# Another order of ScalarE's tasks around the block products of a mixture-of-experts layer

## Chip, cores and metric

The kernel runs on one core of one Trainium2 chip. The metric is the device time of one execution in microseconds (us), and the time before is the median of three runs.

## What is computed

Eight heads of retention (attention without softmax, with a decay matrix) over a batch of 8 sequences of 576 tokens make 4608 rows of 512 numbers. A router then sends each row to one of 8 experts, and each expert is a two-layer network. The second part fills the half of the program that this case is about.

```python
def _moe_ref(x, expert_emb, tau, w1, w2):        # x 4608x512, w1 8x512x1024, w2 8x1024x512
    ...
    expert_idx = np.argmax(logits, axis=1)
    ...
    for e in range(E):
        mask = expert_idx == e
        h = np.maximum(x[mask] @ w1[e], 0.0)
        out[mask] = gate_w[mask, None] * (h @ w2[e])
```

## The kernel before

**Stages.** The first 187 us compute retention, routing and the first layer of expert 0. From there the program alternates, expert by expert, between two stages that TensorE does back to back. The second layer of an expert (`mm2`, line 1150) goes over five tiles of 128 tokens, 24 matmuls each. The first layer of the next expert (`product`, line 1099) is a **block** of 28 block products of six matmuls each: 1 to 7 by block scheme, for each of four weight chunks, seven products in place of eight, in the hand-written sequence `ORDER`. Blocks 1 to 7 belong to experts 1 to 7. Every number is held as a high and a low part, so each operand is split before use: ScalarE casts the high part (line 999 for weights, 399 for tokens) and VectorE subtracts it for the low part (lines 1002 and 403).

**Accumulators.** Products 1, 6, 7 and 4 of one chunk add into the same PSUM tile `Y`. After products 1, 6 and 7 ScalarE copies the sum so far out of `Y` (`follow`, line 1115), and the next product of that chunk must not start before this copy is done. In `ORDER`, product 1 of chunk 0 stands at place 1 and product 6 of chunk 0 at place 5; product 7 of chunk 3 stands at place 25 and product 4 of chunk 3 at place 27. What is copied gets VectorE's additions (line 1111) and goes through the ReLU into `hs`, again as high (line 1070, ScalarE) and low (line 1065, VectorE).

**Weights.** The first layer's weights come in four chunks per expert. Three quarters of a chunk are used as they are (its **own** part, 768 columns). GpSimd makes four **sums** of its blocks (`w1sum`, line 1024, 1024 columns) into the one buffer `wsum`. Both parts are split, `w1hi`/`w1lo` with True for the own part and False for the sums. A chunk's sums may overwrite `wsum` only when the split of the chunk before has read it. The second layer's four chunks are split by `w2hi`/`w2lo`. All these chunks pass through two buffers (raw_72 and raw_78), and `wload` starts the next load in a buffer, on SP's queue, once VectorE has done `w2lo` or the own `w1lo` there.

**Tokens.** GpSimd gathers the five token tiles of the expert after next. For each one ScalarE makes a 16-bit copy (`xturn`, line 357, 128x1024), after which SP issues a DMA that transposes it (line 358). In the next second-layer stage ScalarE joins the halves (`xjoin`, line 364), VectorE forms sums (lines 375 to 382), and both split.

**What sets the order.** All engines run a hand-written order. `mm2_plan` lists what is done in the second-layer stage at its 15 steps (three per tile: after matmul 8, after matmul 16, and after the tile's eviction, line 1159, and its scatter to `out`, line 1160). `mm1_plan` lists what is done after the 1st to 28th product. Each engine works off its queue in this order, and the instruction at the head of a queue holds back all behind it.

Of the kernel before, what the change touches and what calls it, by code (L numbers as in the profile page):

```python
# [84 lines left out]
def retention_moe(ctx: ExitStack, tc: tile.TileContext, qk, kv, w1, w2, head, cst, out):  # L85
# [872 lines left out]
    with ExitStack() as moe:  # L958
# [218 lines left out]
        def mm2_plan(e):  # L1177
            n = e + 1
            if n == NE:
                return {0: [(count_beyond,)]}  # L1180
            plan = {
                0: [(xjoin, n, 0)],
                1: [(xsums, n, 0), (xhigh, n, 0), (w1sum, n, 0)],
                2: [(xlow, n, 0), (w1hi, n, 0, True), (xjoin, n, 1)],
                3: [(xsums, n, 1), (w1lo, n, 0, True), (xhigh, n, 1)],
                4: [(xlow, n, 1), (w1hi, n, 0, False), (xjoin, n, 2)],
                5: [(xsums, n, 2), (w1lo, n, 0, False), (xhigh, n, 2), (w1sum, n, 1)],
                6: [(xlow, n, 2), (w1hi, n, 1, True), (xjoin, n, 3)],
                7: [(xsums, n, 3), (w1lo, n, 1, True), (xhigh, n, 3)],
                8: [(xlow, n, 3), (w1hi, n, 1, False), (xjoin, n, 4)],  # L1190
                9: [(xsums, n, 4), (w1lo, n, 1, False), (xhigh, n, 4), (w1sum, n, 2)],
                10: [(xlow, n, 4), (w1hi, n, 2, True)],
                11: [(w1lo, n, 2, True), (w1hi, n, 2, False)],
                12: [(w1lo, n, 2, False)],
            }
            if n + 1 < NE:
                for i in range(CT):
                    plan[2 + 2 * i].append((gather, n + 1, i))
                plan[12].append((xturn, n + 1, 0))
                plan[14] = [(xturn, n + 1, 1)]  # L1200
            if e == 0:
                plan[0] = [(xturn, 1, 4)] + plan[0]
                plan[12] += [(gather_gates, 1)]
            return plan

        def mm1_plan(e):
            n = e + 1
            plan = {
                2: [(w2hi, e, 0)],
                3: [(w2lo, e, 0), (w1sum, e, 3)],  # L1210
                10: [(w2hi, e, 1)],
                11: [(w2lo, e, 1)],
                12: [(w1hi, e, 3, True)],
                13: [(w1lo, e, 3, True), (w1hi, e, 3, False)],
                15: [(w1lo, e, 3, False)],
                17: [(w2hi, e, 2)],
                18: [(w2lo, e, 2)],
                22: [(w2hi, e, 3)],
                23: [(w2lo, e, 3)],
            }  # L1220
            if n < NE:
                for i, k in ((2, 6), (3, 19), (4, 24)):
                    plan[k] = [(xturn, n, i)]
                plan[9] = [(gather_gates, n)]
            return plan

        b = B - 1
# [13 lines left out]
        for i in range(3):  # L1241
# [4 lines left out]
        plan = {  # L1246
            4: [(w2hi, 0, 0), (gates_exp,)],
            5: [(w2lo, 0, 0), (w2hi, 0, 1)],
            6: [(gates_sum,), (xprep, 0, 3), (xprep, 0, 4)],
            7: [(w2lo, 0, 1)],  # L1250
            8: [(gates_out,)],
            9: [(w2hi, 0, 2), (gather, 1, 3), (gather, 1, 4)],
            10: [(w2lo, 0, 2), (xturn, 1, 0)],
            11: [(w2hi, 0, 3)],
# [9 lines left out]
        for e in range(NE):  # L1264
            if e:
                plan = mm1_plan(e)
                for k, (n, i) in enumerate(ORDER, 1):
                    product(e, n, i)
                    follow(n, i)
                    run_tasks(plan, k)  # L1270
                settle_last()
                settle_last()
            plan = mm2_plan(e)
            for i in range(CT):
                if e * CT + i == NA - 1:
                    ntile = nc.values_load(ovt[0:1, 0:1], min_val=0, max_val=NO)
                mm2(e, i, lambda k: run_tasks(plan, 3 * i + k))
# [186 lines left out]
```

## Time and profile before

| | |
|---|---|
| median of three runs | 603.17 us (602.69 to 603.18) |
| profiled execution | 606.0 us, span 604.2 us |
| busy in the span: TensorE (PE) | 573.9 us, 95% |
| VectorE (DVE) | 407.6 us, 67% |
| ScalarE (ACT) | 384.7 us, 64% |
| GpSimd (POOL) | 309.3 us, 51% |
| granted TensorE clock | 0.995 |

One execution is profiled; it took 1.8 us more than its span, and 2.8 us more than the median. All times of rows are us from the start of the span. Matmuls are pipelined and their ends are modelled, so the time that a stall costs TensorE is read better from the length of a block than from the busy share.

### The profile page before, as it was taken

What the parts mean: (1) busy time and instruction counts of PE and PEld (TensorE: products, weight loads), DVE (VectorE), ACT (ScalarE), POOL (GpSimd) and SP (SyncE); (2) the same over time, 40 slices, a digit from 0 to 9 for tenths busy, and PEclk for the clock granted to TensorE, in tenths of its full rate; (3) what the DMA queues carried; (4) which work ended last, traced back from release to release, by engine and by line L of the source; (5) the groups of instructions that cost most, each with busy time, mean ns of one, the idle gap of its engine ahead of it and who ended that gap; (6) DMA issues with size and microseconds to landing.
All of it is one profiled execution on the core that took longest, in us unless ns stands there. A gap on an engine that the chain in (4) does not pass through costs nothing.

```text
span 604.2 us, 13056 instructions
## 1 busy us (share of the span) xinstructions
PE 573.9 (95%) x5096; PEld 510.5 (84%) x5096; DVE 407.6 (67%) x829; ACT 384.7 (64%) x718; POOL 309.3 (51%) x303
## 2 busy tenths in 40 slices
PE   8999999998999988998998999899989989999996
PEld 7788888887898878888887988888888879889985
DVE  3565777665775857685966868686868768687800
ACT  1344556554557868768877878687587778786511
POOL 4554544454346586378257635933782575245011
PEclk9999999998999999999999999999999999999999
DMA  9999999953467575437735655644376366533201
GB/s 327 395 333 345 382 369 353 395 186 94 152 189 178 168 166 132 119 126 173 172 104 156 168 122 170 160 132 126 116 172 160 104 181 156 117 105 99 69 36 46
DMA packets 72385, 109.58 MB, mean 181 GB/s; under 512 B 42330, under 2 KB 44030, under 8 KB 70528
## 3 DMA queue, kind: packets, MB, share of 16 engines
q1 hardware_dynamic: 62976, 86.53, 47.2%
q0 software_dynamic: 7680, 19.95, 10.3%
q10 hardware_dynamic: 1664, 2.23, 1.1%
q8 instruction: 41, 0.67, 0.4%
q14 instruction: 24, 0.20, 0.1%
HBM read 80.62 MB, written 19.94 MB: 166 GB/s over the span
## 4 chain that ended last, share of the span: by engine, by line
PE 41%; ACT 18%; DVE 18%; issue 13%; POOL 5%; DMA 4%; ACTq 0%; POOLq 0%; DVEq 0%
PE m L1150 9%; PE a L1099 5%; PE a L626 5%; PE m L709 4%; POOL wsum L1024 4%; ACT raw L364 4%; PE a L413 3%; PE m L790 3%; PE m L1099 3%; ACT raw L357 3%; DVE raw L375 2%; DVE hs L1065 2%; ACT hs L1070 2%; PE m L653 2%; DVE y L1111 2%
## 5 line engine op out<-in xcount | busy, mean ns | idle before, releaser
L1150 PE MATMUL m<-w2s,hs 128*128 128x512 f32 (+1 forms) x984 | 219.6, 384 | 0.0
L1150 PEld LDWEIGHTS m<-w2s,hs 128*128 128x128 f32 x984 | 181.2, 188 | 36.0
L1160 POOL DMA_INDIRECT out<-y,sid x40 | 48.0, 1200 | 97.8 <-ACT y L1159 85.2
L1024 POOL TENSOR_TENSOR wsum<-raw 128x256 f32<-128x256 f32 x56 | 47.4, 870 | 62.5 <-DMA raw<-w 25.8
L615 POOL TENSOR_TENSOR qkt<-qkt,gsb 128x448 f32<-128x448 f32 x32 | 37.0, 1174 | 58.5 <-PE a L626 47.7
L1099 PE MATMUL a<-xsb,w0s 128*128 128x320 f32 x324 | 56.7, 314 | 10.0 <-ACT y L1115 9.8
L1099 PEld LDWEIGHTS a<-xsb,w0s 128*128 128x128 f32 x324 | 49.0, 188 | 13.4 <-ACT y L1115 12.7
L1002 DVE TENSOR_TENSOR w2s<-raw,w2s 128x1024 fp32r<-128x1024 f32 x32 | 41.0, 1280 | 19.9 <-issue 10.9
L319 POOL DMA_INDIRECT raw<-xd,gid x40 | 39.4, 985 | 27.3 <-DVE xsb L403 16.8
L330 POOL DMA_INDIRECT gt<-gd,gid x40 | 43.7, 1092 | 18.3 <-issue 10.2
L1070 ACT ACTIVATE hs<-y 128x320 fp32r<-128x320 f32 x84 | 38.7, 472 | 22.4 <-DVE y L1111 20.8
L1111 DVE TENSOR_TENSOR y<-m,y 128x320 f32<-128x320 f32 x84 | 39.1, 484 | 18.1 <-ACT y L1115 15.0
L399 ACT CAST xsb<-raw 128x128 fp32r<-128x128 f32 x70 | 32.1, 459 | 27.5 <-DVE raw L382 26.5
L635 DVE TENSOR_TENSOR raw<-a,cd 128x512 f32<-128x512 f32 x64 | 39.9, 683 | 13.6 <-PE a L626 12.6
L375 DVE TENSOR_TENSOR raw<-raw 128x256 f32<-128x256 f32 x35 | 19.7, 562 | 43.1 <-ACT raw L364 41.3
L1065 DVE SCALAR_TENSOR_TENSOR hs<-y,hs 128x320 fp32r<-128x320 f32 x84 | 46.1, 563 | 3.3 <-ACT hs L1070 1.4
L1159 ACT ACTIVATE y<-m,gt 128x512 f32<-128x512 f32 (+1 forms) x41 | 27.5, 671 | 32.1 <-PE m L1150 32.1
L403 DVE TENSOR_TENSOR xsb<-raw,xsb 128x128 fp32r<-128x128 f32 x70 | 46.9, 702 | 1.1 <-ACT xsb L399 0.6
L364 ACT COPY raw<-raw 128x1024 uint16<-128x1024 uint16 x35 | 47.4, 1353 | 0.0
L1115 ACT COPY y<-a 128x320 f32<-128x320 f32 x84 | 34.9, 425 | 7.7 <-PE a L1099 3.8
L999 ACT CAST w2s<-raw 128x1024 fp32r<-128x1024 f32 x32 | 33.6, 1049 | 6.8 <-DMA raw<-w 6.6
L1099 PE MATMUL m<-xsb,w0s 128*128 128x320 f32 x216 | 37.6, 309 | 0.0
(176 smaller groups left out, 1117.6 us busy)
## 6 DMA issues: line engine op xcount, KB each, us to landing
raw<-w SPq DMA_DIRECT2D x64, 512.0 KB
qkt<-qk SPq DMA_DIRECT2D x28, 576.0 KB
xd<-y SPq DMA_DIRECT2D x36, 256.0 KB
vt<-kv SPq DMA_DIRECT2D x7, 1152.0 KB
kt<-kv SPq DMA_DIRECT2D x7, 1024.0 KB
qkt<-qk ACTq DMA_DIRECT2D x4, 288.0 KB
qkt<-qk SPq DMA_DIRECT2D x4, 288.0 KB
raw<-xd,gid POOLq DMA_INDIRECT x40
```

The lines of the kernel that those rows point to most:

```text
L330: nc.gpsimd.indirect_dma_start(out=g[:, i : i + 1], out_offset=None, in_=gd[:, :], in_offset=bass.IndirectOffsetOnAxis(ap=gid[:, a : a + 1 ...
L364: nc.scalar.copy(far.bitcast(U16).rearrange("p (n h) -> p h n", h=2), near.rearrange("p (h n) -> p h n", h=2))
L403: nc.vector.tensor_tensor(out=lo, in0=u, in1=hi.bitcast(F32), op=ALU.subtract)
L635: nc.vector.tensor_tensor(out=pm[:, h], in0=ps[h].rearrange("p (c n) -> p c n", c=NCH), in1=decay[:, 2 * p + h].unsqueeze(1).broadcast_to( ...
L1002: nc.vector.tensor_tensor(out=lo, in0=u, in1=hi.bitcast(F32), op=ALU.subtract)
L1024: nc.gpsimd.tensor_tensor(out=o, in0=x, in1=y, op=op)
L1065: nc.vector.scalar_tensor_tensor(out=lo, in0=part(src), scalar=0.0, in1=hi.bitcast(F32), op0=ALU.max, op1=ALU.subtract)
L1070: nc.scalar.activation(hi, part(src), AF.Relu)
L1099: nc.tensor.matmul(ps[:, :HC], w[:, ws, ka, d * P : (d + 1) * P], xop(kx, xsp)[:, d, :], start=(n in (1, 2, 5) and d == 0 and k == 0), sto ...
L1111: nc.vector.tensor_tensor(out=out[:, :HC], in0=x[:, :HC], in1=out[:, :HC], op=ALU.add)
L1150: nc.tensor.matmul(ps[:, :step], hs[:, hsp, f, i * P : (i + 1) * P], w[:, ws, f, n : n + step], start=(j == 0 and k == 0), stop=(j == NF - ...
L1160: put = nc.gpsimd.indirect_dma_start(out=out[:, :], out_offset=bass.IndirectOffsetOnAxis(ap=sid[:, a : a + 1], axis=0), in_=y, in_offset=None,
```

## The change

Two tables of places are rewritten; no instruction is added or taken out, and TensorE's order is the same before and after. In the second-layer stage the split of the third chunk's sums leaves (its high part from step 11, its low part from step 12). Three 16-bit copies of token tiles take steps 10, 11 and 12; before, there were two, at steps 12 and 14.

```diff
                 10: [(xlow, n, 4), (w1hi, n, 2, True)],
-                11: [(w1lo, n, 2, True), (w1hi, n, 2, False)],
-                12: [(w1lo, n, 2, False)],
+                11: [(w1lo, n, 2, True)],
             }
...
-                plan[12].append((xturn, n + 1, 0))
-                plan[14] = [(xturn, n + 1, 1)]
+                for i in range(3):
+                    plan.setdefault(10 + i, []).append((xturn, n + 1, i))
```

In the block, `mm1_plan` gets that split at places 2 and 3, and the rest is spread anew:

```diff
             plan = {
-                2: [(w2hi, e, 0)],
-                3: [(w2lo, e, 0), (w1sum, e, 3)],
...
+                2: [(w1hi, e, 2, False)],
+                3: [(w1lo, e, 2, False)],
+                5: [(w1sum, e, 3)],
```

| task in the block | place before | place after |
|---|---|---|
| w2 chunk 0, high / low | 2 / 3 | 6 / 7 |
| sums of w1 chunk 3 (GpSimd) | 3 | 5 |
| w2 chunk 1, high / low | 10 / 11 | 14 / 15 |
| w1 chunk 3 own, high / low | 12 / 13 | 12 / 13 |
| w1 chunk 3 sums, high / low | 13 / 15 | 16 / 17 |
| w2 chunk 2, high / low | 17 / 18 | 19 / 20 |
| w2 chunk 3, high / low | 22 / 23 | 24 / 25 |
| token copies (xturn) | tiles 2, 3, 4 at 6, 19, 24 | tiles 3, 4 at 10, 28 |

ScalarE's queue from the end of expert 0's second layer into block 1, before (w0s and wsa hold split w1 weights, w2s the split w2, raw_73 to raw_77 the token tiles, y_79 to y_83 the rows to be scattered and, in a block, the copies out of `Y`):

```order
L999 CAST w0s<-raw_78 128x768
L1159 ACTIVATE y_82<-m,gt 128x512
L999 CAST w0s<-wsum 128x1024
L357 COPY raw_73<-raw_73 128x1024
L1159 ACTIVATE y_83<-m,gt 128x512
L357 COPY raw_74<-raw_74 128x1024
L1115 COPY y_79<-a 128x320
L999 CAST w2s<-raw_72 128x1024
L1070 ACTIVATE hs<-y_79 128x5x64
L1115 COPY y_80<-a 128x320
```

The same stretch after:

```order
L999 CAST w0s<-raw_78 128x768
L357 COPY raw_73<-raw_73 128x1024
L1159 ACTIVATE y_82<-m,gt 128x512
L357 COPY raw_74<-raw_74 128x1024
L357 COPY raw_75<-raw_75 128x1024
L1159 ACTIVATE y_83<-m,gt 128x512
L1115 COPY y_79<-a 128x320
L999 CAST w0s<-wsum 128x1024
L1070 ACTIVATE hs<-y_79 128x5x64
L1115 COPY y_80<-a 128x320
L1115 COPY y_81<-a 128x320
L999 CAST w2s<-raw_72 128x1024
```

The cast of `wsum`, which reads GpSimd's sums, stood four instructions ahead of the first copy out of `Y` (line 1115) and now stands right behind it.

ScalarE's queue at places 11 to 19 of block 1, before:

```order
L1070 ACTIVATE hs<-a 128x5x64
L999 CAST wsa<-raw_78 128x768
L1115 COPY y_79<-a 128x320
L1070 ACTIVATE hs<-y_81 128x5x64
L999 CAST wsa<-wsum 128x1024
L1070 ACTIVATE hs<-y_79 128x5x64
L1070 ACTIVATE hs<-y_80 128x5x64
L1070 ACTIVATE hs<-a 128x5x64
L1115 COPY y_83<-a 128x320
L999 CAST w2s<-raw_72 128x1024
L1115 COPY y_80<-a 128x320
L357 COPY raw_76<-raw_76 128x1024
```

After:

```order
L1070 ACTIVATE hs<-a 128x5x64
L999 CAST wsa<-raw_78 128x768
L1115 COPY y_79<-a 128x320
L1070 ACTIVATE hs<-y_81 128x5x64
L1070 ACTIVATE hs<-y_79 128x5x64
L999 CAST w2s<-raw_72 128x1024
L1070 ACTIVATE hs<-y_80 128x5x64
L1070 ACTIVATE hs<-a 128x5x64
L999 CAST wsa<-wsum 128x1024
L1115 COPY y_83<-a 128x320
L1115 COPY y_80<-a 128x320
L999 CAST w2s<-raw_78 128x1024
```

The second w2 chunk (raw_72) now stands here, the cast of the fourth chunk's sums moved down to just ahead of the copy of place 17 (y_83), and the third w2 chunk is now read from raw_78, the buffer that the own part of w1 chunk 3 left.

ScalarE's queue at the end of block 1, before:

```order
L1115 COPY y_81<-a 128x320
L1070 ACTIVATE hs<-y_82 128x5x64
L999 CAST w2s<-raw_78 128x1024
L1070 ACTIVATE hs<-a 128x5x64
L357 COPY raw_77<-raw_77 128x1024
L1115 COPY y_79<-a 128x320
L1070 ACTIVATE hs<-y_79 128x5x64
L1070 ACTIVATE hs<-y_83 128x5x64
L1070 ACTIVATE hs<-a 128x5x64
L1070 ACTIVATE hs<-y_81 128x5x64
```

After:

```order
L1115 COPY y_81<-a 128x320
L1070 ACTIVATE hs<-y_82 128x5x64
L1070 ACTIVATE hs<-a 128x5x64
L999 CAST w2s<-raw_72 128x1024
L1115 COPY y_79<-a 128x320
L1070 ACTIVATE hs<-y_79 128x5x64
L1070 ACTIVATE hs<-y_83 128x5x64
L1070 ACTIVATE hs<-a 128x5x64
L357 COPY raw_77<-raw_77 128x1024
L1070 ACTIVATE hs<-y_81 128x5x64
```

One 16-bit copy (line 357) left the stretch ahead of the copy of place 25 (y_79) and now stands ahead of the block's last ReLU.

## Rows read from the trace of the kernel before

**Rows 1.** Waits of TensorE from 187 us on: total us, times, longest

```profile
PE a L1099 <- ACT y L1115: 15.4, 14, 2.5
```

**Rows 2.** Busy time by window, blocks 1 to 7: window, length, PE, PEld, DVE, ACT, POOL

```profile
213.31:243.70 30.39, 25.99 (x170) 24.68 (x168) 20.52 (x33) 22.12 (x40) 23.13 (x23) 1.00 0.63 155
270.93:298.47 27.54, 25.38 (x169) 24.70 (x168) 19.95 (x32) 22.23 (x40) 16.60 (x17) 1.00 0.70 169
325.69:352.85 27.16, 25.18 (x170) 24.65 (x168) 20.22 (x32) 22.18 (x40) 16.78 (x17) 1.00 0.70 165
380.08:408.81 28.73, 25.92 (x170) 24.68 (x169) 20.46 (x32) 22.16 (x40) 17.30 (x18) 1.00 0.64 159
436.04:463.63 27.59, 25.44 (x169) 24.66 (x168) 20.28 (x32) 22.18 (x40) 16.88 (x18) 1.00 0.64 163
490.86:518.37 27.51, 25.34 (x169) 24.65 (x168) 20.29 (x32) 22.30 (x40) 16.76 (x18) 1.00 0.69 172
545.60:570.33 24.73, 24.73 (x170) 24.65 (x168) 19.57 (x32) 17.92 (x35) 7.10 (x8) 1.00 0.34 102
```

**Rows 3.** Timeline of TensorE, block 3, places 4, 5 and 27: start, length, [idle before]

```profile
328.35 1.04 PE L1099 MATMUL a<-xsa,wsa 128*128 128x320 f32 x6
331.08 1.15 PE L1099 MATMUL a<-xsb,w0s 128*128 128x320 f32 x6 [1.69 <-ACT y L1115]
...
350.98 1.15 PE L1099 MATMUL a<-xsb,w0s 128*128 128x320 f32 x6 [0.29 <-ACT y L1115]
```

**Rows 4.** Timeline of ScalarE from the second layer into block 3

```profile
322.34 0.83 ACT L999 CAST w0s<-raw 128x768 fp32r<-128x768 f32 x1
323.07 0.68 ACT L1159 ACTIVATE y<-m,gt 128x512 f32<-128x512 f32 x1
327.19 1.05 ACT L999 CAST w0s<-wsum 128x1024 fp32r<-128x1024 f32 x1 [3.43 <-POOL wsum L1024]
328.14 1.04 ACT L357 COPY raw<-raw 128x1024 uint16<-128x1024 uint16 x1
...
330.60 0.42 ACT L1115 COPY y<-a 128x320 f32<-128x320 f32 x1
```

**Rows 5.** Timeline of GpSimd, last of the third chunk's sums, ahead of block 3

```profile
325.82 1.34 POOL L1024 TENSOR_TENSOR wsum<-raw,wsum 128x256 f32<-128x256 f32 x1
```

**Rows 6.** Timeline of ScalarE, start of block 7

```profile
547.10 1.05 ACT L999 CAST w0s<-wsum 128x1024 fp32r<-128x1024 f32 x1 [3.43 <-POOL wsum L1024]
...
548.64 0.42 ACT L1115 COPY y<-a 128x320 f32<-128x320 f32 x1
```

**Rows 7.** Timeline of ScalarE, end of block 7

```profile
567.89 0.42 ACT L1115 COPY y<-a 128x320 f32<-128x320 f32 x1 [0.57 <-PE a L1099]
...
571.05 0.47 ACT L1070 ACTIVATE hs<-y 128x320 fp32r<-128x320 f32 x1 [0.79 <-DVE y L1111]
```

**Rows 8.** Timeline of ScalarE, first eviction of the second layer behind block 2

```profile
304.13 0.69 ACT L1159 ACTIVATE y<-m,gt 128x512 f32<-128x512 f32 x1 [1.45 <-PE m L1150]
```

**Rows 9.** Timeline of VectorE, block 7, low part of w1 chunk 3 (own)

```profile
558.56 0.95 DVE L1002 TENSOR_TENSOR wsa<-raw,wsa 128x768 fp32r<-128x768 f32 x1
```

**Rows 10.** Timeline of SP's queue, issue of the load of w2 chunk 2, blocks 2 and 4

```profile
285.67 2.60 SPq L991 DMA_DIRECT2D raw<-w  x2
...
395.18 0.38 SPq L991 DMA_DIRECT2D raw<-w  x1
```

**Rows 11.** Timeline of ScalarE, high part of that chunk, blocks 2 and 4

```profile
289.40 1.07 ACT L999 CAST w2s<-raw 128x1024 fp32r<-128x1024 f32 x1
...
400.00 1.05 ACT L999 CAST w2s<-raw 128x1024 fp32r<-128x1024 f32 x1 [1.18 <-DMA raw<-w]
```

**Rows 12.** Timeline of ScalarE, block 1, copy of place 10

```profile
227.95 0.43 ACT L1115 COPY y<-a 128x320 f32<-128x320 f32 x1 [2.12 <-issue]
```

**Rows 13.** Timeline of TensorE, block 1, place 16

```profile
230.76 2.03 PE L1099 MATMUL a<-xsb,w0s 128*128 128x320 f32 x12 [1.33 <-ACT y L1115]
```

**Rows 14.** Timeline of GpSimd, block 1, last of the fourth chunk's sums

```profile
229.07 0.73 POOL L1024 TENSOR_TENSOR wsum<-raw,wsum 128x256 f32<-128x256 f32 x1
```

More of the change, by code (lines that the diff above doesn't have):

```diff
@@ L1198, in mm2_plan @@
                     plan[2 + 2 * i].append((gather, n + 1, i))
-                plan[12].append((xturn, n + 1, 0))
-                plan[14] = [(xturn, n + 1, 1)]
+                for i in range(3):
+                    plan.setdefault(10 + i, []).append((xturn, n + 1, i))
             if e == 0:
                 plan[0] = [(xturn, 1, 4)] + plan[0]
-                plan[12] += [(gather_gates, 1)]
+                plan[12].append((gather_gates, 1))
             return plan
@@ L1208, in mm1_plan @@
             plan = {
-                2: [(w2hi, e, 0)],
-                3: [(w2lo, e, 0), (w1sum, e, 3)],
-                10: [(w2hi, e, 1)],
-                11: [(w2lo, e, 1)],
-                12: [(w1hi, e, 3, True)],
[L1214 to L1219, printed above, removed]
+                2: [(w1hi, e, 2, False)],
+                3: [(w1lo, e, 2, False)],
+                5: [(w1sum, e, 3)],
+                6: [(w2hi, e, 0)],
+                7: [(w2lo, e, 0)],
+                12: [(w1hi, e, 3, True)],
+                13: [(w1lo, e, 3, True)],
+                14: [(w2hi, e, 1)],
+                15: [(w2lo, e, 1)],
+                16: [(w1hi, e, 3, False)],
+                17: [(w1lo, e, 3, False)],
+                19: [(w2hi, e, 2)],
+                20: [(w2lo, e, 2)],
+                24: [(w2hi, e, 3)],
+                25: [(w2lo, e, 3)],
             }
             if n < NE:
-                for i, k in ((2, 6), (3, 19), (4, 24)):
-                    plan[k] = [(xturn, n, i)]
                 plan[9] = [(gather_gates, n)]
+                plan[10] = [(xturn, n, 3)]
+                plan[28] = [(xturn, n, 4)]
             return plan
```

## The prediction

> **What bounds the kernel now.** I read the wait list of TensorE first. From 187 us on TensorE waits for one thing alone, ScalarE's copies out of `Y`: 14 waits, 15.4 us [rows 1]. Then I cut the trace into the seven blocks. Each holds the same 28 products, yet blocks 1 to 6 take 27.16 to 30.39 us and block 7 takes 24.73, in which TensorE is never idle [rows 2]. Block 7 is followed by no further tokens, so its ScalarE queue holds no 16-bit copies. 24.73 us is what 28 products cost without a wait, 0.883 a place, and I take it as the floor of a block. Against it blocks 2 to 6 lose 2.81, 2.43, 4.00, 2.86 and 2.78, together 14.88 us, and block 1 loses 5.66. So 20.5 us at most lie open. ScalarE is busy 22 of some 27 us in a block [rows 2]: its order is the fault, more than its amount of work.
>
> Where the loss sits is read in block 3. Place 5 starts 2.73 us after place 4 instead of 0.883 later, and place 27 has another short wait [rows 3]. ScalarE's timeline tells why: after the eviction at 323.07 it idles 3.43 us for GpSimd's sums, then casts them, makes two 16-bit copies and an eviction, and only at 330.60 takes the first copy out of `Y` [rows 4]. The sums are ready at 325.82 + 1.34 = 327.16 [rows 5]. The wait for the sums alone would not hurt: block 7 has it too, with the same cast behind it, but there the copy out of `Y` comes at 548.64, 3.04 us after the block's start, against 4.91 in block 3 [rows 2, 4, 6]. The two 16-bit copies make the difference.
>
> **Part 1: the start of a block.** In block 3's times, the own cast ends at 322.34 + 0.83 = 323.17 [rows 4]. Now follow a 16-bit copy (1.04), the eviction (0.68), two more copies (2.08), the last eviction (0.68) and the copy out of `Y` (0.42): 323.17 + 4.90 = 328.07, without a wait, since the matmuls of the second layer end with the block's start at 325.69. Place 5 is due at 328.35 + 0.88 = 329.23 [rows 3, 4]. So 1.16 us are to spare and the first wait goes. The cast of the sums comes right behind, at 328.1, when they have been ready for 0.9 us. Its result is first used at place 15, twelve us later. The three copies need gathers that GpSimd issues in steps 2, 4 and 6, six steps or more ahead. Of their transposing DMAs the first stands in SP's queue ahead of the load released at step 11; its copy ends 1.04 us after the own cast, and the subtraction that releases the load takes 0.95 [rows 4, 9], so it holds the load back by 0.1 at most. The other two stand behind that load.
>
> **Part 2: the middle of the block.** Three places carry a risk.
> - Place 16: the cast of the fourth chunk's sums (1.05) now stands ahead of the copy of place 17. GpSimd begins these sums two places later, after the split at places 2 and 3; at four operations of 0.73 to 1.34 us [rows 5, 14] they take 3 to 5 of the 9.7 us from place 5 to place 16, and cost nothing, except in block 1 (below).
> - Place 14: the second w2 chunk is asked for after place 7 instead of 3 and read after 14 instead of 10, the same seven places. I cost it at nothing.
> - Place 19: the third w2 chunk goes into the buffer that the own part of w1 chunk 3 leaves. In block 7 that subtraction ends at 558.56 + 0.95 = 559.51, 13.9 us into the block [rows 2, 9]. The load takes 3.73 us at most in block 2 and 4.82 in block 4, where ScalarE idled for it [rows 10, 11]. So it lands at 17.6 to 18.7; with the cast (1.05) and the copy of place 20 (0.42) this ends at 19.1 to 20.2. Place 23 needs that copy and is due at 22 x 0.883 = 19.4. The price is 0 to 0.8 us a block. I take 0.2, since of blocks 1 to 6 only block 4 shows a wait there; 1.0 for blocks 2 to 6.
>
> **Part 3: the end of the block.** The 16-bit copy ahead of the copy of place 25 is gone. Block 7 has the order that remains, and there ScalarE is idle 0.57 us before that copy and no wait follows [rows 2, 7]. So the second wait goes too. In exchange a copy of 1.04 now stands ahead of the block's last ReLU, where block 7 shows 0.79 idle [rows 4, 7], and VectorE subtracts the last w2 chunk after the addition of place 25 instead of before (estimate 1.27, rows 9 scaled from 768 to 1024 columns). At worst the ReLU and all token work behind it slip by 1.04 + 1.27 - 0.79 = 1.5 us. That is covered by ScalarE's 1.45 idle ahead of the next second layer's first eviction [rows 8]; what is left over, 0.1, eats into the 1.16 to spare in part 1. Without this cover each block would lose up to 0.3.
>
> **Part 4: block 1.** Here GpSimd runs late, with ten small gathers in its queue, and its clock is not moved by the change. Its fourth sums end at 229.07 + 0.73 = 229.80 [rows 14]. The cast and the copy of place 17 then end near 231.3, and place 20, due at 213.31 + 19 x 0.883 = 230.1, loses 1.2: a gain of 5.66 - 1.2 = 4.4. But ScalarE also idled 2.12 us until 227.95, for something that the trace doesn't show, and place 16 began only at 230.76 [rows 12, 13]. If that event keeps its time, as the same copies stand behind it, the block's last 13 places end at 230.76 + 11.5 = 242.2, and the gain is 243.70 - 242.2 = 1.5. I take 1.5: a DMA's or GpSimd's time is the nearest explanation, and neither moves.
>
> One rule of the Trainium skill speaks against the late sums. In the rows the same fourth operation of the sums takes 1.34 us ahead of block 3, and 0.73 in block 1 [rows 5, 14]. "SBUF — State Buffer", section "SBUF: two separate sides", says that VectorE and GpSimd share one port pair and that a VectorE operation with two SBUF inputs and a GpSimd operation shut each other out for their whole length; the two durations agree with that. By it the fourth sums, now beside the subtractions of places 3 and 7, could end some 1.2 us later, and the far end of block 1's gain would be 3.2 instead of 4.4.
>
> **The sum.** 14.88 - 1.0 for blocks 2 to 6, plus 1.5 for block 1: 15.4 us. The profiled execution of 606.0 us would become 590.6 (span 588.8), and the median of 603.17, 2.8 lower, 587.8. Block 7 and the first 187 us don't move.
>
> **The rivals.**
> - *All of it goes* (0.20). The load lands early and block 1 keeps none of its gap: 14.88 + 4.4 = 19.3, 583.9; with block 1 at the floor too, 582.6. For it: block 7 shows a whole block without a wait. Against: block 1's rows.
> - *The third w2 chunk is late in every block* (0.14). At 4.82 us the price is 0.8 in each of six blocks, 4.8 instead of 1.0: 591.6. For it: block 4 [rows 10, 11]. Against: block 2. The page "DMA: Bandwidth & Descriptors", section "Issuing engines are not separate DMA queues", says that DMAs of all queues interleave on the same 16 engines, so a load next to transposing DMAs would be longer; no row here separates them.
> - *The first wait stays in part* (0.08). If the token work slips by a us more than part 3 says, the copy out of `Y` misses place 5 by about 1 us in five blocks: 587.8 + 5 = 592.8. Against: two covers in a row.
> - *The waits only change their place* (0.03). The casts put off to places 2 to 7 push every later copy, and the blocks stay near 27 us: 603. Against: the count of ScalarE's tasks in a block is as before, 22 of 27 us.
> - *Slower* (0.03). The load for place 19 decides: a length of 4.0 us just fits (13.9 + 4.0 + 1.05 + 0.42 = 19.4), and from 7.4 us on it costs more than the 3.4 us a block that are lost now (20.5 over six). At 9 us each block would be 5.0 late, 1.6 more than now: 603.2 + 6 x 1.6 = 612.8. Against: no load here shows more than 4.82.
>
> **How the numbers follow.** The forecast, with blocks of 24.8 to 25.5 and block 1 near 29, has 0.52. Its time is 587.8. The range of 8 in 10 reaches from 583.0 (all but the very floor) to 592.5 (late loads and most of the partly kept wait). 0.2% of the time is 1.2 us, about what a measurement of this kernel can tell from no change. Faster: 0.52 + 0.20 + 0.14 + 0.08 = 0.94; same 0.03; slower 0.03.
>
> **What would show it.** Right: blocks 2 to 6 below 25.5 us; no TensorE wait at place 5; ScalarE without idle time between the own cast of the third chunk and the first copy out of `Y`; the cast of the sums behind it. Wrong: a wait of TensorE at places 20 or 23 with ScalarE waiting for a DMA (part 2), at place 27 (part 3), or at place 5 with late token work (part 3); in block 1 a start of place 16 well before 230 would show that the 1.5 was too careful.

## The result, and the profile after

The changed kernel takes 594.76 us (median; 603.17 before). The ratio of the two, run beside each other, is 0.9838, with a 95% interval of 0.9802 to 0.9874: 9.8 us less, between 7.6 and 11.9. It is faster, as forecast, but the forecast was 15.4 us, and 594.76 lies above the range of 583.0 to 592.5. The ratio leaves out one slow execution, the profiled one of 602.03 us, which the median still holds; the five others took 590.65 to 595.34 us. In a second set of runs beside the experiments the ratio was 0.9806 (0.9759 to 0.9853).

The profiled execution of after ran at a lower granted clock at its start (0.89 in the first 20 us and 0.94 in the next 20, against 1.00 before), and its block 1 starts 5.85 us later. So only lengths from there on, all at a granted clock of 1.00, are compared; after_again, below, shows the same losses in an execution of 593.69 us. The seven blocks, as in [rows 2] (window, its length, busy time and count on PE, PEld, DVE, ACT, POOL, granted clock, DMA share, GB/s):

```profile
219.16:248.00 28.84, 25.44 (x170) 24.66 (x168) 20.42 (x31) 18.48 (x35) 22.08 (x20) 1.00 0.52 150
275.23:302.23 27.00, 25.75 (x170) 24.68 (x169) 19.60 (x31) 18.48 (x35) 14.97 (x15) 1.00 0.65 161
329.45:354.88 25.43, 25.07 (x170) 24.65 (x169) 19.83 (x31) 18.48 (x35) 15.66 (x15) 1.00 0.63 168
382.10:408.40 26.30, 25.79 (x170) 24.66 (x169) 20.84 (x31) 18.69 (x35) 15.39 (x15) 1.00 0.58 161
435.63:461.50 25.87, 25.19 (x170) 24.66 (x169) 20.18 (x31) 18.57 (x35) 15.91 (x15) 1.00 0.56 159
488.71:514.49 25.78, 25.33 (x170) 24.70 (x169) 19.64 (x31) 18.47 (x35) 14.95 (x15) 1.00 0.64 171
541.72:566.37 24.65, 24.65 (x170) 24.65 (x169) 19.46 (x31) 17.44 (x33) 7.83 (x8) 1.00 0.31 103
```

Blocks 2 to 6 went from 138.53 to 130.38 us, 8.15 less, and block 1 from 30.39 to 28.84, 1.55 less: 9.7 together, the measured gain. Above five floors of 24.73 us blocks 2 to 6 still lose 6.73, where the forecast left 1.0. ScalarE's busy time in a block fell from 22.2 to 18.5 us, as three copies now lie in the second layer. The waits of TensorE from 187 us on, as in [rows 1]:

```profile
PE a L1099 <- ACT y L1115: 6.1, 10, 2.3
```

What each place takes over 0.883 us tells where they lie. It is worked out from the start of each product's first weight load (PEld), from 0.05 us on, without the 0.09 that every block loses at its first product. The place behind a wait gives about 0.04 back, so the entries add up to a little more than the block loses:

| block | place 5 | 12 to 16 | 20 | 23 | 27 |
|---|---|---|---|---|---|
| 1 | 0 | 0 | 2.59 | 1.05 | 0.66 |
| 2 | 0 | 1.34 | 0.44 | 0.05 | 0.66 |
| 3 | 0 | 0 | 0.09 | 0.15 | 0.66 |
| 4 | 0 | 0.52 | 0.44 | 0.21 | 0.66 |
| 5 | 0 | 0 | 0 | 0.60 | 0.67 |
| 6 | 0 | 0.14 | 0.41 | 0 | 0.65 |
| 7 | 0 | 0 | 0 | 0 | 0 |

The wait at place 5 is gone in all blocks. The one at place 27 is there in six, and the middle has new ones. TensorE in block 3, places 4, 5 and, further down, 26 to 28, as in [rows 3] (start, length, idle before and what ended it):

```profile
332.11 1.04 PE L1099 MATMUL a<-xsa,wsa 128*128 128x320 f32 x6
332.98 1.04 PE L1099 MATMUL a<-xsb,w0s 128*128 128x320 f32 x6
...
351.60 1.04 PE L1099 MATMUL m<-xsb,w0s 128*128 128x320 f32 x6
353.00 1.15 PE L1099 MATMUL a<-xsb,w0s 128*128 128x320 f32 x6 [0.36 <-ACT y L1115]
353.99 1.04 PE L1099 MATMUL m<-xsb,w0s 128*128 128x320 f32 x6
```

ScalarE's timeline of the same block, its start (against [rows 4]) and then the stretch from place 9 on:

```profile
328.35 1.98 ACT L357 COPY raw<-raw 128x1024 uint16<-128x1024 uint16 x2
330.24 0.68 ACT L1159 ACTIVATE y<-m,gt 128x512 f32<-128x512 f32 x1
330.82 0.41 ACT L1115 COPY y<-a 128x320 f32<-128x320 f32 x1
331.12 1.06 ACT L999 CAST w0s<-wsum 128x1024 fp32r<-128x1024 f32 x1
...
338.69 0.43 ACT L1115 COPY y<-a 128x320 f32<-128x320 f32 x1 [1.51 <-DMA out<-y,sid]
339.01 0.47 ACT L1070 ACTIVATE hs<-y 128x320 fp32r<-128x320 f32 x1
339.39 0.42 ACT L1115 COPY y<-a 128x320 f32<-128x320 f32 x1
339.69 1.06 ACT L357 COPY raw<-raw 128x1024 uint16<-128x1024 uint16 x1
340.64 0.45 ACT L1070 ACTIVATE hs<-a 128x320 fp32r<-128x320 f32 x1
340.97 0.84 ACT L999 CAST w0s<-raw 128x768 fp32r<-128x768 f32 x1
...
347.43 1.05 ACT L999 CAST w2s<-raw 128x1024 fp32r<-128x1024 f32 x1 [0.64 <-DMA raw<-w]
...
350.89 0.47 ACT L1070 ACTIVATE hs<-y 128x320 fp32r<-128x320 f32 x1 [0.75 <-DVE y L1111]
351.27 0.42 ACT L1070 ACTIVATE hs<-a 128x320 fp32r<-128x320 f32 x1
351.59 1.04 ACT L999 CAST w2s<-raw 128x1024 fp32r<-128x1024 f32 x1
352.52 0.43 ACT L1115 COPY y<-a 128x320 f32<-128x320 f32 x1
```

At the start of the block all is as predicted: no idle time, the copy out of `Y` 1.37 us after the block's start and the sums' cast right behind it. Three things then add up. The copy of place 9 waits 1.51 us for the landing of the scatter of the fourth token tile, whose rows lie in the same buffer: no such wait stood in the profile before, and over the blocks there are five, 8.4 us. Behind it stands the 16-bit copy of place 10, then eleven tasks with gaps of 0.49 us in all. The third w2 chunk, whose load comes 0.64 us later still, is cast 17.98 us into the block, and the last one, at place 24, so late that the copy of place 25 ends after place 27 is due.

Block 7 has the same casts at the same places, but no 16-bit copy at place 10, and loses nothing there. The same cast of the third chunk, the cast at place 24 and the copy behind it:

```profile
558.92 1.05 ACT L999 CAST w2s<-raw 128x1024 fp32r<-128x1024 f32 x1 [0.49 <-DMA raw<-w]
...
563.08 1.04 ACT L999 CAST w2s<-raw 128x1024 fp32r<-128x1024 f32 x1
564.01 0.43 ACT L1115 COPY y<-a 128x320 f32<-128x320 f32 x1
```

The copy starts 22.29 us after the block's start, in block 3 23.07: 0.78 later, of which 0.66 become a wait.

### The profile page after: what moved, and what is told of

It reads as the page before. It is cut to its first block, busy times and chain, and to the rows that moved or that the text cites. A ratio compares the mean times of both kernels' runs of the same rounds, so it can differ in the third digit from the quotient of the medians.

```text
span 600.2 us, 13042 instructions
## 1 busy us (share of the span) xinstructions
PE 577.8 (96%) x5096; PEld 512.5 (85%) x5096; DVE 413.7 (69%) x829; ACT 384.7 (64%) x718; POOL 317.4 (53%) x303
## 3 DMA queue, kind: packets, MB, share of 16 engines
q10 hardware_dynamic: 1664, 2.23, 1.1%
## 4 chain that ended last, share of the span: by engine, by line
PE 52%; ACT 13%; DVE 13%; DMA 11%; issue 9%; POOL 2%; SPq 0%; POOLq 0%; ACTq 0%; DVEq 0%
PE m L1150 21%; PE a L626 5%; PE a L1099 5%; DMA raw<-w 4%; PE m L709 4%; PE a L413 3%; DMA out<-y,sid 3%; PE m L1099 3%; PE m L790 3%; DVE hs L1065 2%; DMA cd<-cst 2%; ACT y L1115 2%; PE m L653 2%; ACT w0s L999 2%; ACT raw L364 2%
## 5 line engine op out<-in xcount | busy, mean ns | idle before, releaser
L1024 POOL TENSOR_TENSOR wsum<-raw 128x256 f32<-128x256 f32 x56 | 50.7, 926 | 61.6 <-DMA raw<-w 42.0
L1111 DVE TENSOR_TENSOR y<-m,y 128x320 f32<-128x320 f32 x84 | 40.8, 486 | 34.7 <-ACT y L1115 32.4
L319 POOL DMA_INDIRECT raw<-xd,gid x40 | 39.4, 986 | 27.2 <-DVE xsb L403 16.8
L1002 DVE TENSOR_TENSOR w2s<-raw,w2s 128x1024 fp32r<-128x1024 f32 x32 | 42.8, 1337 | 0.0
L626 PE MATMUL a<-qkt 64*128 64x128 f32 x512 | 36.5, 290 | 3.3 <-DVE raw L635 2.2
L626 PEld LDWEIGHTS a<-qkt 64*128 64x128 f32 x512 | 32.6, 196 | 6.5 <-issue 3.3
```

Source lines behind the costliest of these rows:

```text
L626: nc.tensor.matmul(ps[h][:, c * P : (c + 1) * P], t[hs, 1, c * P : (c + 1) * P], t[hs, 0, c * P : (c + 1) * P], start=True, stop=True,)
L1002: nc.vector.tensor_tensor(out=lo, in0=u, in1=hi.bitcast(F32), op=ALU.subtract)
L1024: nc.gpsimd.tensor_tensor(out=o, in0=x, in1=y, op=op)
L1111: nc.vector.tensor_tensor(out=out[:, :HC], in0=x[:, :HC], in1=out[:, :HC], op=ALU.add)
```

## The experiments

All kernels were timed against the kernel before on the same chip; the executions differ by some us in the first stretch, which no edit touches (the second layer of expert 0 starts between 182.5 and 191.9 us in the profiles). From there on the second-layer stages between the blocks take 27.2 us in every kernel (27.65 once, in best), so what an edit does shows in the blocks. Their lengths, from traces, decide wherever the ratios lie within each other's intervals. "Blocks 2 to 6" is their loss above five floors of 24.73, by windows as above; before it is 14.88, and block 1 took 30.39. They come from one execution of each kernel, and that has its own spread: gates_only changes nothing in blocks 2 to 6 against after and after_again, and the three lose 4.74, 6.73 and 7.15 there. Differences of some 2 us in this column show nothing by themselves.

| kernel | ratio (95% interval) | blocks 2 to 6, us | block 1, us |
|---|---|---|---|
| after | 0.9838 (0.9802 to 0.9874) | 6.73 | 28.84 |
| after_again | 0.9806 (0.9759 to 0.9853) | 7.15 | 28.78 |
| split_only | 0.9911 (0.9878 to 0.9945) | 12.07 | 30.31 |
| copies_only | 1.0002 (0.9973 to 1.0030) | 15.57 | 28.58 |
| copies3 | 0.9867 (0.9813 to 0.9921) | 9.48 | 28.41 |
| chunk4_22 | 0.9894 (0.9848 to 0.9940) | 9.93 | 30.59 |
| turn3_26 | 0.9763 (0.9721 to 0.9805) | 0.90 | 30.70 |
| gather_12 | 0.9819 (0.9770 to 0.9869) | 5.62 | 28.98 |
| lo_12 | 0.9859 (0.9810 to 0.9907) | 5.71 | 31.43 |
| turn3_13 | 0.9809 (0.9767 to 0.9851) | 4.03 | 29.03 |
| gates_only | 0.9821 (0.9782 to 0.9860) | 4.74 | 25.92 |
| turn3_26_gates | 0.9666 (0.9618 to 0.9714) | 1.29 | 24.84 |
| t3_gates_again | 0.9733 (0.9692 to 0.9774) | 1.61 | 24.73 |
| extra_copy | 0.9762 (0.9731 to 0.9792) | 4.93 | 25.17 |
| best | 0.9748 (0.9700 to 0.9797) | 2.69 | 28.31 |

**Which half of the change gives the gain.** Two kernels have one half each. The first keeps the new places of splits and weight chunks and puts the 16-bit copies back:

```diff
-                for i in range(3):
-                    plan.setdefault(10 + i, []).append((xturn, n + 1, i))
+                plan[12] = [(xturn, n + 1, 0)]
+                plan[14] = [(xturn, n + 1, 1)]
...
-                plan[10] = [(xturn, n, 3)]
-                plan[28] = [(xturn, n, 4)]
+                for i, k in ((2, 6), (3, 19), (4, 24)):
+                    plan.setdefault(k, []).append((xturn, n, i))
```

> From the changed kernel the five 16-bit copies go back to where they stood before (steps 12 and 14 of the second layer, places 6, 19 and 24); the splits and the weight chunks keep their new places. Theory (the copies must be out of the block): the wait at place 5 stays away, worth 2.0 us in each of blocks 2 to 6, but at place 24 a cast and a copy (1.04 each) now stand ahead of the copy of place 25, so place 27 loses about 1.7 us instead of 0.66 in six blocks, and place 20 or 23 loses some tenths more: 597 to 601 us. Rival (moving the split alone carries the gain): about 593.4, as the changed kernel. If the bunched transposing DMAs are what delays the scatter of the fourth token tile, the wait of the copy of place 9 for that scatter (8.4 us in five blocks of the changed kernel) is gone here.

As the theory said: place 5 loses nothing, and place 27 loses 1.5 to 1.7 us in five of the six blocks (0.4 in block 6, which has lost 2.2 us at place 20 by then). The scatter's wait did not go (8.6 us in five blocks), so it doesn't need the transposing DMAs in one bunch.

The second is the kernel before with the copies moved, and the split of the third sums behind them but still ahead of the block:

```diff
-                11: [(w1lo, n, 2, True), (w1hi, n, 2, False)],
-                12: [(w1lo, n, 2, False)],
+                11: [(w1lo, n, 2, True)],
+                12: [],
+                13: [(w1hi, n, 2, False), (w1lo, n, 2, False)],
...
+                for i in range(3):
+                    plan.setdefault(10 + i, []).append((xturn, n + 1, i))
```

> From the kernel before only the 16-bit copies move, as in the change (steps 10, 11 and 12, place 10, place 28); the split of the third weight sums stays ahead of the block, behind the three copies, and the weight chunks stay. Theory: the copies alone fill ScalarE's wait for the sums. By block 3's old times the copies end at 326.97, the sums at 327.16, the cast at 328.2, the eviction at 328.9 and the copy out of Y at 329.3, against 329.23 for place 5: 0 to 0.3 us a block stay of 2.0. The last weight chunk is cast after place 22 with no copy behind it, so place 27 loses nothing, and no cast of sums stands ahead of the copy of place 17: 587 to 591 us. Rival (the split had to leave the start of the block): place 5 still loses a us or more in every block, 595 to 600.

Half of this was right: place 5 loses 0.1 in blocks 2 to 6 (0.9 in block 1). The time was wrong, for place 16 loses up to 2.9 and place 22 up to 1.6 us. ScalarE in its block 3 shows the same three things as in the changed kernel, in a queue where four casts stand closer together (copy of place 9, second w2 chunk, the 16-bit copy of place 10, own cast, cast of the sums):

```profile
335.89 0.43 ACT L1115 COPY y<-a 128x320 f32<-128x320 f32 x1 [2.29 <-DMA out<-y,sid]
...
337.62 1.05 ACT L999 CAST w2s<-raw 128x1024 fp32r<-128x1024 f32 x1 [0.62 <-DMA raw<-w]
338.57 1.04 ACT L357 COPY raw<-raw 128x1024 uint16<-128x1024 uint16 x1
...
339.85 0.82 ACT L999 CAST w0s<-raw 128x768 fp32r<-128x768 f32 x1
...
341.26 1.04 ACT L999 CAST w0s<-wsum 128x1024 fp32r<-128x1024 f32 x1
```

So either half removes the first wait alone, and neither is worth the whole: what a half leaves out comes back further down the queue.

**Place 27: the cast at place 24, or what makes the queue late.** Two edits of the changed kernel:

```diff
-                24: [(w2hi, e, 3)],
-                25: [(w2lo, e, 3)],
+                22: [(w2hi, e, 3)],
+                23: [(w2lo, e, 3)],
```

> The changed kernel with one edit: the fourth chunk of w2 is split after places 22 and 23 again instead of 24 and 25. Theory A (the cast at place 24 took the room of the 16-bit copy that left, ahead of the copy of place 25): the 0.66 us at place 27 goes in six blocks, 4.0 us: 589.4. Rival (the queue is late since the third chunk of w2 lands late, whatever stands there): the cast of 1.04 only pushes the copies behind it, place 25 or 27 still loses about 0.6, and the time stays at 593.

Theory A falls. Place 27 still loses 0.3 to 0.7 in five blocks, and place 28 now loses 0.53 in all but block 3 (0.22), for an addition of VectorE that stands behind the earlier subtraction; block 7, at the floor before, takes 25.14 us. The waits of TensorE:

```profile
PE a L1099 <- ACT y L1115: 6.9, 9, 3.2
PE m L1099 <- DVE y L1111: 1.6, 6, 0.3
```

The other edit moves the one 16-bit copy that the change had put into the middle of the block:

```diff
-                plan[10] = [(xturn, n, 3)]
+                plan[26] = [(xturn, n, 3)]
```

> The changed kernel with one edit: the 16-bit copy of the fourth token tile stands after place 26 instead of place 10. Theory D (the copy at place 10 delays the own part of the fourth weight chunk, with it the load of the third w2 chunk, and through its cast, the subtraction and one addition the cast at place 24; block 7, without that copy, splits the same chunks at the same places and loses nothing at place 27): the load is released about 0.6 us earlier, place 27 loses 0.1 or less instead of 0.66 and place 20 nothing: 5 to 6 us, 588. Rival A (the cast at place 24 is the cause by itself): place 27 keeps 0.66, 592 to 593. A price at the other end may show: two copies ahead of the second layer's first eviction.

Theory D's result: blocks 2 to 6 come within 0.9 us of their five floors, with the cast at place 24 where it was. The third w2 chunk is cast 17.2 to 18.2 us into these blocks, 18.0 to 19.6 in the changed kernel; in both ScalarE waits for its load there, but for one block of turn3_26 or two. So the copy's time also reaches the end of the block by way of that load, which starts when the own part of the fourth weight chunk is split. No price shows at the other end.

```profile
272.14:297.76 25.62, 25.36 (x170) 24.68 (x168) 19.41 (x31) 18.49 (x35) 15.85 (x15) 1.00 0.64 159
324.99:349.67 24.68, 24.68 (x169) 24.63 (x168) 19.77 (x31) 18.53 (x35) 15.54 (x15) 1.00 0.59 162
376.90:401.56 24.66, 24.66 (x170) 24.65 (x169) 19.89 (x31) 18.66 (x35) 15.46 (x15) 1.00 0.57 161
428.79:453.65 24.86, 24.86 (x170) 24.67 (x169) 20.04 (x31) 18.61 (x35) 15.59 (x15) 1.00 0.54 155
480.87:505.60 24.73, 24.73 (x170) 24.64 (x169) 19.68 (x31) 18.41 (x35) 15.56 (x15) 1.00 0.63 168
```

The same move in the kernel with the copies alone:

```diff
-                plan.setdefault(10, []).append((xturn, n, 3))
+                plan[26] = [(xturn, n, 3)]
```

> The kernel before with the 16-bit copies moved as in the change, the third split still ahead of the block, but the fourth copy after place 26 instead of place 10. The run with it at place 10 gained nothing: place 5 lost only 0.1, but places 16, 20 and 22 lost 2 us. Theory D (the 16-bit copy at place 10 and not the places of the splits makes those waits): places 16 and 22 lose 0.5 or less, 588 to 592 by the clock of the first runs, a ratio of 0.975 to 0.982. Rival (the splits must be spread as in the change, since the scatter holds the copy of place 9 and four casts stand close behind): place 16 keeps 1 us or more, ratio 0.99 to 1.00.

Between the two: 6 us of block losses go, the ratio falls by 0.0135, yet place 16 keeps 0.5 to 1.3 us in four blocks and place 28 0.52 in six. With the copy at place 26 in both, the split inside the block and the spread chunks are worth 8.6 us in blocks 2 to 6 (9.48 against 0.90).

**The scatter, the load, or ScalarE's time.** The changed kernel once more, and then with GpSimd's gather behind the scatter instead of ahead of it:

> The changed kernel, as it is, on the same chip and beside the same runs of the kernel before as the next three, so that small differences can be read. All theories: a ratio near 0.984, blocks 2 to 6 at 25.4 to 27.0 us, place 27 losing 0.66 in blocks 1 to 6 and nothing in block 7.

```diff
                 for i in range(CT):
-                    plan[2 + 2 * i].append((gather, n + 1, i))
+                    plan.setdefault(2 + 2 * i if i < 4 else 12, []).append((gather, n + 1, i))
```

> The changed kernel with one edit on GpSimd's queue alone: the gather of the last token tile of the next expert is issued at step 12 of the second layer instead of step 10, so that the scatter of the fourth token tile no longer stands behind it. Theory C (the copy of place 9 waits for that scatter's landing, 8.4 us in five blocks, and this pushes places 13, 16 and 20): the scatter starts 1.3 us earlier, the wait falls to 2 to 4 us, the losses at places 12 to 20 of blocks 2 to 6 (3.4 us in all) to 1 or less, while place 27 keeps most of its 0.66, since the 16-bit copy of place 10 still stands ahead of the own part: 2 to 3 us less than the changed kernel. Rival (the other DMAs decide when the scatter lands, not when it is issued): no difference.

The second profile of the changed kernel has the same losses at the same places (0.63 to 0.67 at place 27 in blocks 2 to 6; 0.15 in block 1, which lost more before). The gather's move takes the scatter's wait from 9.9 to 3.5 us, but only 1.5 us of the losses of blocks 2 to 6, 1.1 of it ahead of place 17; place 27 keeps 0.65 in four of them. The ratios can't be told apart, and 1.5 us lie within the spread of single executions. The stronger evidence is turn3_26: its copies of place 9 wait 10.8 us for the scatter in all, and blocks 2 to 6 lose 0.90. The scatter is a wait that ScalarE mostly makes good where the 16-bit copy doesn't stand behind it.

Next the load of the third w2 chunk, released earlier by VectorE alone:

```diff
-                12: [(w1hi, e, 3, True)],
-                13: [(w1lo, e, 3, True)],
+                12: [(w1hi, e, 3, True), (w1lo, e, 3, True)],
```

> The changed kernel with one pair of VectorE's instructions swapped in each block: the subtraction of the own part of the fourth weight chunk, which releases the load of the third w2 chunk, goes ahead of the addition of place 13 instead of behind it. ScalarE's order is untouched, the 16-bit copy stays at place 10. Theory D by the load (the release of that load, and not ScalarE's time, is what ends last): the load is released up to 0.9 us earlier, its cast no longer waits, and place 27 loses 0.2 or less instead of 0.66 and place 23 nothing, in blocks 2 to 6: 3 to 5 us less than the changed kernel, ratio 0.972 to 0.977. Rival (ScalarE's queue as a whole is one copy too late behind place 10): place 27 keeps 0.6, ratio 0.981 to 0.984.

Neither theory as put. Places 23 and 27 lose nothing, but place 20 loses 0.8 to 1.0 in each of blocks 2 to 6. The addition now behind the subtraction holds a ReLU of ScalarE by 0.73 us (the row names the subtraction ahead of it), and the cast of the third chunk, without waiting, stands 18.02 us into the block, where it stood 17.98 with its wait for the load:

```profile
341.32 0.47 ACT L1070 ACTIVATE hs<-y 128x320 fp32r<-128x320 f32 x1 [0.73 <-DVE w0s L1002]
...
344.89 1.07 ACT L999 CAST w2s<-raw 128x1024 fp32r<-128x1024 f32 x1
```

Load and queue are late by the same amount, and freeing one shows the other. (Block 1, at 31.43, is the subject of the last section.)

```diff
-                plan[10] = [(xturn, n, 3)]
+                plan[13].append((xturn, n, 3))
```

> The changed kernel with the fourth 16-bit copy after place 13, right behind the own cast of the fourth weight chunk and its neighbours, instead of after place 10, right ahead of them. ScalarE's work between places 9 and 16 stays the same, the load of the third w2 chunk is released about 0.6 us earlier. Theory D by the load: place 27 falls to 0.25 or less as with the copy at place 26; place 20 keeps 0.4 to 1.0, as the cast of the sums is no earlier: 1 to 3 us less than the changed kernel. Rival (ScalarE's queue): place 27 stays at 0.66 and the time is unchanged.

Inconclusive in time: place 27 loses 0.05, 0.41, 0.67, 0.67 and 0.31 in blocks 2 to 6, and their sum is 3.1 below that of the changed kernel beside it in this section, while the ratio is the same.

The last test puts ScalarE's 1.04 us back without the DMA. Its base has the copy at place 26 and block 1's edit, below:

```diff
-    def xturn(e, i):
+    def xturn(e, i, turn=True):
...
+        if turn:
...
+                plan[10] = [(xturn, n, 3, False)]
                 plan[26] = [(xturn, n, 3)]
```

> The kernel with the fourth 16-bit copy after place 26 and block 1's gate gathers behind the sums, with one thing added: at place 10 ScalarE makes that 16-bit copy once more, without its transposing DMA, so the copy is made twice and the DMAs stand as in the kernel without the addition. Theory (ScalarE's 1.04 us in the stretch from place 9 to place 20 is the cause): the losses of the changed kernel come back, 0.4 to 0.7 at place 27 and 0.1 to 0.5 at place 20 in most of six blocks, 4 to 6 us over the same kernel without it. Rival (the transposing DMA in the middle of the block delays the loads and the scatter): blocks stay within 0.3 of the kernel without it, 1 us or less.

> The kernel with the fourth 16-bit copy after place 26 and block 1's gate gathers behind the sums once more, beside the run with the copy doubled. Theory: blocks 1 to 6 lose 0.1 to 1.2 us each against 28 products of 0.883 us, ratio to the kernel before 0.965 to 0.972. Rival (the first run of it was a lucky one): ratio 0.975, with losses as in the run of the three edits together.

The losses come back: 0.56 to 0.66 at place 27 in all six blocks, 0.29 to 0.44 at place 20 in three. TensorE's waits, of the kernel with the copy made twice (one line further down in the code), and of its base:

```profile
PE a L1100 <- ACT y L1116: 2.1, 7, 0.4
```

```profile
PE a L1099 <- ACT y L1115: 0.8, 2, 0.6
```

Blocks 1 to 6 are 3.8 us longer together (4.93 + 25.17 against 1.61 + 24.73), the medians 3.1 (588.73 against 585.63), a little under the 4 to 6 expected; the intervals of the ratios overlap, and the evidence is the return of the losses at their places, place 27 in all six blocks. In blocks 2 to 6 4.93 is also what gates_only loses with the transposing DMA in place, 4.74: the DMA's share can't be seen there (block 1 is 0.75 longer with it). So it is ScalarE's time in the stretch from place 9 to place 20.

**Block 1.** The sums that block 1 waits for stand behind five gathers of gates in GpSimd's queue. One edit puts these behind the sums, alone and together with the copy's move:

```diff
-                plan[12].append((gather_gates, 1))
...
                 plan[9] = [(gather_gates, n)]
+                if e == 1:
+                    plan[6].append((gather_gates, 1))
```

> The changed kernel with only block 1's edit: expert 1's five gate gathers behind the sums of the fourth weight chunk. Theory: block 1 loses no more at place 20 and falls to the length of blocks 2 to 6, from 28.9 to about 26 us: 3 us less, ratio 0.976; blocks 2 to 6 as in the changed kernel. Rival (block 1's losses only move to the third w2 load and place 23): less than 1.5 us.

> The changed kernel with the fourth 16-bit copy after place 26, and in block 1 the five small gathers of expert 1's gates issued after place 6, behind the sums of the fourth weight chunk, instead of ahead of them at step 12. Theory (block 1 waits for GpSimd: the five gathers take 7.3 us, the sums start at 229.2, and place 20 loses 4.2 us): the sums start near 221, the loss at place 20 goes, block 1 falls from 31 to about 26 us and the time by 4 us against the run with the copy alone at place 26: ratio 0.968 to 0.971. Rival (another wait stands close behind, the third w2 load or the scatter): 1 to 2 us alone.

Both as the theory said for the block: 28.8 to 25.92 alone, and 24.84, a tenth above the floor, with the copy moved. In the time the edit alone can't be told from the changed kernel (0.9821, where 0.976 was expected; the profiled execution, at 589.55 us, was the fastest of six with a median of 595.69). The two together are the fastest kernel here, at 0.9666 and, run again, 0.9733, medians of 584.40 and 585.63 us. They beat both kernels. Against gates_only this is the copy's move alone, and here the ratios show it without the traces: 0.9782 to 0.9860 with the copy at place 10, 0.9618 to 0.9714 and 0.9692 to 0.9774 with it at place 26.

All three edits:

> The three edits together: fourth 16-bit copy after place 26, expert 1's gate gathers behind the sums in block 1, last token gather at step 12. Against the run with the first two: what is left in blocks 2 to 6 is 0.5 at place 13 in block 2 (scatter) and 0.1 to 0.5 at place 27. Theory: the scatter's part goes, 0 to 1 us less, ratio 0.964 to 0.967. Rival: no difference that can be measured, since ScalarE has idle time behind place 9 in these blocks.

It is not the best: blocks 2 to 6 lose 2.69, and block 1 loses 2.55 us at place 27, in a wait of ScalarE and TensorE for which the trace names nothing of this core. Whether that comes with the edit stays open; the scatter's part gave nothing.

## Why the prediction was right and wrong

- **Part 1, the start of a block: right.** No wait at place 5 in any block. The copy out of `Y` ends 1.75 us ahead of place 5, 1.16 were worked out. The two half kernels show that it was overdetermined: either half does it.
- **Part 2, place 19: right in its sum.** Place 23 loses 1.01 us in blocks 2 to 6 together; 1.0 was taken. That it fits so well is luck: 0.60 of it fell in block 5, and only 0.21 in block 4, which the prediction took it from.
- **Part 2, place 16: right only by itself.** The cast of the sums ahead of the copy of place 17 cost 1.38 us in blocks 2 to 6, not nothing; but with the copy of place 10 away it costs 0.4 in one block, at the same place. The step is not at fault.
- **Part 2 left a place out; this is the step that failed.** Of the five 16-bit copies the prediction followed those that leave, the three at the start of the block and the one at its end. The one that came new into the middle, after place 10, has no price in it. It takes 1.06 us in the one stretch where ScalarE has no slack, and is worth 5.8 us in blocks 2 to 6 (6.73 against 0.90) by its removal, 3.5 where both kernels have block 1's edit (4.74 against 1.29), and 3.8 in six blocks by putting its time alone back. The forecast left 1.0 for all losses of blocks 2 to 6.
- **Part 3, the end of the block: wrong for the same reason.** "Block 7 has the order that remains" was true of the casts near place 25 and not of what stands ahead of them: blocks 1 to 6 have a task of 1.04 us more, 14 places earlier, and are 0.78 late at the copy of place 25. Block 7 was the wrong floor for a stretch that isn't the same in it. The bounds of 1.5 us for the tasks behind the block never came into play.
- **A wait behind the wait.** Once the copies out of `Y` come on time, the copy of place 9 meets the scatter of the tile that used its buffer. This could have been read before: the buffer's name is in the order, the scatter's issue in GpSimd's timeline. Its price is small: 1.5 us by gather_12, no more than single executions differ by.
- **Part 4, block 1: the size right by luck, the reason not.** 1.55 us came, 1.5 were taken. But the unnamed event of [rows 12] is not what stayed; ScalarE in block 1 waits for GpSimd's sums (2.99 us), then for the third w2 load (1.96). The sums ended 16.49 us into the block [rows 14], now 17.72. The two casts in ScalarE's timeline, and the sums in GpSimd's:

```profile
236.91 1.04 ACT L999 CAST wsa<-wsum 128x1024 fp32r<-128x1024 f32 x1 [2.99 <-POOL wsum L1024]
...
240.57 1.05 ACT L999 CAST w2s<-raw 128x1024 fp32r<-128x1024 f32 x1 [1.96 <-DMA raw<-w]
```

```profile
232.53 1.73 POOL L1024 TENSOR_TENSOR wsum<-raw 128x256 f32<-128x256 f32 x2
234.23 0.99 POOL L1024 TENSOR_TENSOR wsum<-wsum,raw 128x256 f32<-128x256 f32 x1
235.30 1.58 POOL L1024 TENSOR_TENSOR wsum<-raw,wsum 128x256 f32<-128x256 f32 x1
```

The last operation takes 1.58 us, 0.73 before. This agrees with the rule that the prediction weighed, from the Trainium skill, "SBUF — State Buffer", section "SBUF: two separate sides": VectorE and GpSimd lock each other out of a shared port pair. The delay of 1.2 us that was estimated by it is near the one measured, 1.23: the four operations began 13.4 us into the block, 13.5 before, and took 4.35 us in place of 2.96. VectorE's subtraction of a w2 chunk beside them took 1.76 us, 1.21 in block 3. No run here shows the lock apart from other causes.

The two rivals that lay nearest are not what happened either: ScalarE waits for the third w2 load in every block, but place 23 loses that rival's 0.8 in none of blocks 2 to 6 (0.60 at most, in block 5), and the first wait left nothing.

## What to carry to other kernels

When tasks are moved in a queue that is full, follow each one to where it lands, and price it there first: a task that leaves two places and enters a third can give back at the third what it won. A stretch without waits in another stage is a floor for this one only if the tasks ahead of it are the same, as far back as the last idle time. And a wait that vanishes when its cause is eased may only have been covering another of the same length: ease both, or put the suspected time back by itself.

## What the runs showed of the hardware

A wait of TensorE can be followed by a lower clock, and then costs more than its length. In turn3_26 TensorE waited 3.88 us in block 1 until 235.18, and after it ran 2.5 us at a granted clock of 0.58, near the lower of its two levels (1.2 GHz); windows ahead, across, and behind the wait:

```profile
214.20:231.00 16.80, 16.80 (x115) 16.60 (x113) 12.07 (x18) 11.82 (x23) 14.43 (x12) 1.00 0.58 153
231.00:236.00 5.00, 1.12 (x8) 0.85 (x7) 3.71 (x5) 1.70 (x3) 4.47 (x5) 1.00 0.17 43
236.00:238.50 2.50, 2.50 (x13) 2.50 (x12) 0.46 (x2) 1.02 (x2) 1.89 (x3) 0.58 0.88 333
```

A product at the lower level takes up to 0.72 us more, so a part of this block 1's 30.70 us is clock and not waiting. The length of the wait doesn't settle it: the changed kernel's 2.29 us wait in block 1 was followed by full clock, and in after_again one of 2.23 us by 0.50 for 3 us.

A scatter's time to land differs more than twofold within one program; what makes it long was not isolated. The two scatters between 275 and 290 us of the changed kernel took 7.1 us from issue to landing (median), those of the whole program 3.1:

```profile
out<-y,sid POOLq DMA_INDIRECT x2, 7.1
```

```profile
out<-y,sid POOLq DMA_INDIRECT x40, 3.1
```
